# A decode kernel's last twenty microseconds: products ahead of sums, earlier output products, v-stationary tokens and unused matmuls

## The chip, the cores and the metric

The kernel runs on one core of a Trainium2 chip. The metric is the device time of one execution in microseconds (us), quoted as the median of several executions. The profile is of one execution, recorded by the hardware profiler; its "span" is 1.7 to 2.9 us shorter than the device time of the same execution. Points of time inside an execution are counted from the start of the span. The engines are called by their names in the profile: PE is TensorE's matmuls, PEld its weight loads, DVE VectorE, ACT ScalarE, SPq the queue of SyncE, which issues the DMA transfers. The "granted clock" (PEclk) is the share of TensorE's full clock that the throttle let through.

## The reference, cut to what matters

Two attention blocks, A and B, of the same shape, each with one query token, 32 heads, 8192 cached keys and values of 128 elements, all bf16. The outputs are concatenated.

```python
q = (x @ wq)                                     # [32 heads, 128]
scores = einsum("bhqd,bhkd->bhqk", q, k_cache) * 128 ** -0.5
p = softmax(scores)
o = einsum("bhqk,bhkd->bhqd", p, v_cache)
y = o.reshape(1, 1, 32 * 128) @ wo               # wo [4096, 512]
# ... once for A, once for B
out = concatenate([y_A, y_B], axis=-1)
```

The caches are 4 x 67 MB and everything is read once, so the data read decides the time: 285 MB.

## The kernel before: the parts that matter

Heads are taken two at a time: pair j, 0 to 31, of which 16 to 31 are B's. A pair's k (4 MB) and v (4 MB) go through a ring of five slots. For a pair j the kernel makes the elementwise products of k and q on DVE (`plan_M`, eight of 1.2 us), folds 128 elements to 8 on TensorE with an identity (`plan_fold`, two of 16 matmuls), sums the rest on DVE (`plan_R`), finds the maximum, takes the exponentials on ACT, and multiplies with v on TensorE (`plan_PV`). Work of neighbouring pairs is interleaved by hand. Every engine runs its own list in order. This is the order of one pair:

```python
for j in range(NPR):                  # NPR = 32
    plan_M(j, 0); plan_M(j, 1)
    plan_R(j - 1, 1); plan_m1(j - 1)  # second sum and maximum of the pair before
    plan_ri(j - 2)
    plan_M(j, 2); plan_M(j, 3)
    plan_tr(j - 1)
    plan_fold(j, 0)
    plan_ot(j - 2)                    # not for j = 31
    plan_M(j, 4); plan_M(j, 5)
    plan_m2(j - 1); plan_bc(j - 1); plan_exp(j - 1)
    plan_M(j, 6); plan_M(j, 7)
    plan_o(j - 2)                     # not for j = 31
    plan_R(j, 0)
    plan_fold(j, 1)
    plan_sum(j - 1)
    plan_PV(j - 1)                    # not for j = 30 and 31
    if j == LE:                       # LE = 28
        ... plan_w(0, ...)            # the weights of A's y, for each block of heads
        ... plan_y(0, ...)            # A's y: 32 matmuls of 512 columns
    if LE <= j < NPR - 1:
        plan_w_ready(j - 2)           # the weights of B's first 16 heads, for j = 28
```

`plan_PV` has p as the stationary operand and streams v, 4 tokens to a matmul of 512 columns. It needs a copy of its sum by ACT and then a turn on TensorE (`plan_ot`, 4 float32 matmuls that the profile counts as 8). `plan_PVturned` has v as the stationary operand, one token to a matmul of 2 columns, and adds to the turned sum directly. The end of the kernel before:

```python
LAST_PARTS = [(0, 64), (64, 96), (96, 128)]   # v of pair 31 comes in three transfers
NLW = 2                                       # the first two go through plan_PV
# ... behind the loop, j = 31:
plan_PV(j - 2); plan_tr(j); plan_ot(j - 2); plan_m2(j); plan_bc(j); plan_exp(j); plan_o(j - 2)
# ... then 96 matmuls of B's y (24 heads), the rest of the weights, the row sums, 16 more matmuls of y
plan_PV(j - 1)
plan_ot(j - 1)
plan_o(j - 1)
LW = LAST_PARTS[NLW - 1][1]
for i, (t0, t1) in enumerate(LAST_PARTS):
    W('PE', *part_of[i])                      # wait for this transfer
    if t1 <= LW:
        plan_PV(j, t0, t1, LW)
    else:
        if t0 == LW:
            plan_ot(j, False)
        plan_PVturned(j, t0, t1)
    if i == 0:
        plan_ysq(0)                           # y of pair 30's heads: 8 matmuls of 128 columns
plan_o(j)
plan_ysq(1)                                   # y of pair 31's heads, then the cast and the output
```

## Time and profile before

| what | before |
|---|---|
| median (lowest to highest) | 672.63 us (672.29 to 672.79, 3 runs) |
| read | 285.21 MB at 425 GB/s over the span |
| chain that ended last | DMA 62%, PE 24%, DVE 11% |
| last piece of v31 lands | 665.6 us |
| from there to the end of the cast | 3.8 us |

Below are three lines of the page: the span, and the clock and the DMA's busy share in 40 slices of the span, in tenths.

```profile
span 671.3 us, 6004 instructions
...
PEclk9998876779877767888876789877767888798787
DMA  9999999999999999999999999999999999999995
```

The DMA engines are busy throughout, so the stream sets when the last bytes land: in each of the seven profiles in which TensorE waited for the last landing (before, E2, E5 to E8 and E15 below) it came between 665.3 and 665.8 us. The clock row shows a TensorE that is cold (slowed by the throttle) for part of nearly every slice. The profile is of an execution of 673.07 us, 0.3 us above the three timed ones.

The end of the chain of waits of the kernel before, in order of time; the columns are start, length and what it was.

```profile
635.32 30.26 DMA ring<-in_B_v_cache_dram
...
665.62 1.26 PE stps L552 x8
666.89 0.87 PE stps L564 x32
...
667.85 0.19 DVE sq L585
...
668.08 1.03 PE qwps L689 x8
...
669.13 0.28 DVE y_sb L699
```

Here the chain runs back from the cast to a transfer: TensorE waited for the last third of v31. L552 is the turn, L564 the 32 v-stationary matmuls, L689 the output sum.

The windows view of the kernel before shows steps of 4 us; PEclk and the DMA share are the columns ahead of the last.

```profile
core 0: us, PE busy (x) PEld busy (x) DVE busy (x) ACT busy (x) POOL busy (x), PEclk, DMA share, GB/s
652.00:656.00 4.00, 3.70 (x113) 3.40 (x113) 0.52 (x3) 0.99 (x5) 0.00 (x0) 0.58 0.92 385
656.00:660.00 4.00, 3.79 (x33) 1.28 (x25) 0.00 (x0) 0.17 (x1) 0.00 (x0) 0.56 0.97 410
```

And this is the timeline of the kernel before, 65 us earlier, where A's y (L643) is made:

```profile
590.09 7.07 PE L643 MATMUL yps<-ring,w_bf 128*1 128x512 bf16 x32 [1.76 <-DVE w_bf L623]
...
597.68 0.42 DVE L614 TENSOR_TENSOR wt<-qwps,hmask 128x256 f32<-128x256 f32 x1 [7.74 <-PE qwps L607]
...
598.48 2.35 DVE L422 TENSOR_TENSOR ring<-ring,qbc 128x2048 bf16<-128x2048 bf16 x2
```

DVE is idle for 7.74 us. The product that it is waiting for (L607) makes the weights of B's first 16 heads, and it stands behind A's y on TensorE. Only then come the products of pair 29 (L422, 598.48 us), and they do not wait for k of pair 29 either.

### The profile page before, as it was taken

To read this page: it belongs to the slowest core of one execution; us is meant where nothing else is said; L and a number is where in the kernel's file an instruction comes from. 1 tells how busy PE (TensorE), PEld (TensorE's weight loads), DVE (VectorE), ACT (ScalarE), POOL (GpSimd) and SP (SyncE) were. 2 spreads that over 40 slices of the span, in tenths; PEclk is the share of its full clock that TensorE was granted. 3 is DMA by queue.
4 is the path that set the end of the run, shared out by engine and by line. 5 is a ranking of instruction groups with operands and counts; after the bars stand their busy time and mean duration, and the time that the engine had idled before them with its cause. 6 is when DMAs were issued, how large, how long until landed. Compare 5 with 4: busy or idle time off the path is not lost.

```text
span 671.3 us, 6004 instructions
## 1 busy us (share of the span) xinstructions
PE 439.0 (65%) x2782; PEld 102.8 (15%) x1822; DVE 387.5 (58%) x517; ACT 61.9 (9%) x203; POOL 2.4 (0%) x16
## 2 busy tenths in 40 slices
PE   2765775655677666567765655777566567757696
PEld 0200110101111010111111101111011111121134
DVE  5194566665555666555566665556666555555840
ACT  0101101001111001111100011110101111101010
POOL 1000000000000000000000000000000000000000
PEclk9998876779877767888876789877767888798787
DMA  9999999999999999999999999999999999999995
GB/s 375 437 437 433 430 421 431 437 436 432 421 428 437 437 433 430 420 435 437 433 435 428 424 435 437 433 433 422 430 437 435 433 428 424 433 436 429 426 422 240
DMA packets 10953, 285.38 MB, mean 425 GB/s; under 512 B 1211, under 2 KB 1726, under 8 KB 1854
## 3 DMA queue, kind: packets, MB, share of 16 engines
q1 hardware_dynamic: 10936, 285.22, 99.0%
q8 instruction: 8, 0.13, 0.1%
q14 instruction: 3, 0.02, 0.0%
q10 hardware_dynamic: 6, 0.00, 0.0%
HBM read 285.21 MB, written 0.00 MB: 425 GB/s over the span
## 4 chain that ended last, share of the span: by engine, by line
DMA 62%; PE 24%; DVE 11%; issue 2%; SPq 0%; DVEq 0%
DMA ring<-in_B_k_cache_dram 30%; DMA ring<-in_A_k_cache_dram 28%; PE fold L181 15%; DVE ring L422 8%; DMA ring<-in_B_v_cache_dram 5%; PE otps L526 3%; PE fold L177 2%; PE stps L552 1%; DVE s_sb L448 1%; PE yps L643 1%; DVE m L459 1%; PE stps L477 1%; DVE wt L614 0%; DVE w_bf L623 0%; DVE rinv L502 0%
## 5 line engine op out<-in xcount | busy, mean ns | idle before, releaser
L422 DVE TENSOR_TENSOR ring<-ring,qbc 128x2048 bf16<-128x2048 bf16 x256 | 298.4, 1216 | 166.5 <-DMA ring<-in_A_k_cache_dram 93.7
L181 PE MATMUL fold<-ring,ident 128*128 128x512 bf16 x960 | 276.3, 452 | 0.0
L467 PE MATMUL stps<-ident_f,m 128*2 128x128 f32 x32 | 11.1, 348 | 141.7 <-DVE rinv L502 140.2
L177 PE MATMUL fold<-ring,ident 128*128 128x512 bf16 x64 | 31.4, 491 | 64.6 <-DVE ring L422 64.6
L526 PE MATMUL otps<-ring,p 128*8 128x512 bf16 x1016 | 62.7, 387 | 0.2 <-DMA ring<-in_B_v_cache_dram 0.2
L552 PEld LDWEIGHTS stps<-sel,o 128*128 128x128 f32 x256 | 33.6, 192 | 157.3 <-issue 152.1
L448 DVE TENSOR_REDUCE s_sb<-fold 128x64 f32<-128x512 f32 x64 | 44.0, 688 | 3.2 <-PE fold L181 2.6
L483 ACT COPY nb<-stps 128x1 f32<-128x1 f32 x32 | 5.1, 159 | 419.2 <-PE stps L477 419.2
L585 DVE TENSOR_TENSOR ot<-stps,rinv 128x2 f32 (+1 forms) x30 | 4.8, 160 | 62.5 <-PE stps L552 62.5
L552 PE MATMUL stps<-sel,o 128*128 128x2 f32 x256 | 30.9, 243 | 3.1 <-DMA ring<-in_B_v_cache_dram 1.9
L541 ACT COPY o<-otps 128x512 f32<-128x512 f32 x32 | 18.7, 585 | 135.7 <-PE otps L526 135.7
L489 ACT ACTIVATE p<-s_sb,nb 64x128 bf16<-64x128 f32 x64 | 28.0, 437 | 3.8
L496 PEld LDWEIGHTS stps<-rowsum,ones_f 128*128 128x128 f32 x64 | 12.3, 194 | 98.7 <-issue 97.9
L467 PEld LDWEIGHTS stps<-ident_f,m 128*2 128x2 f32 x32 | 2.6, 81 | 158.8 <-DVE m L459 132.0
L526 PEld LDWEIGHTS otps<-ring,p 128*8 128x8 bf16 x1016 | 22.5, 87 | 24.3 <-issue 1.6
L387 PE MATMUL qwps<-ring,xsel 128*128 128x512 bf16 x64 | 18.6, 443 | 9.3 <-ACT qbc L394 4.8
L459 DVE TENSOR_REDUCE m<-s_sb 64x1 f32<-64x128 f32 x64 | 17.9, 280 | 2.1
L177 PEld LDWEIGHTS fold<-ring,ident 128*128 128x128 bf16 x64 | 6.4, 99 | 78.0 <-issue 59.6
L614 DVE TENSOR_TENSOR wt<-qwps,hmask 128x512 f32<-128x512 f32 (+3 forms) x5 | 2.2, 441 | 21.4 <-PE qwps L607 21.3
L477 PE MATMUL stps<-m,sel 2*128 2x1 f32 x64 | 12.1, 256 | 0.0
L489 ACT ACTIVATION_READ_ACCUMULATOR p<-s_sb,nb 64x1 f32 x64 | 11.6, 181 | 0.0
L477 PEld LDWEIGHTS stps<-m,sel 2*128 2x128 f32 x64 | 9.4, 182 | 10.5 <-issue 10.0
(49 smaller groups left out, 80.1 us busy)
## 6 DMA issues: line engine op xcount, KB each, us to landing
ring<-in_A_k_cache_dram SPq DMA_DIRECT2D x16, 4096.0 KB, 39.4
ring<-in_A_v_cache_dram SPq DMA_DIRECT2D x16, 4096.0 KB, 31.9
ring<-in_B_k_cache_dram SPq DMA_DIRECT2D x16, 4096.0 KB, 39.4
ring<-in_B_v_cache_dram SPq DMA_DIRECT2D x15, 4096.0 KB, 32.0
ring<-in_A_wq_dram SPq DMA_DIRECT2D x1, 4096.0 KB, 12.1
ring<-in_B_wq_dram SPq DMA_DIRECT2D x1, 4096.0 KB, 21.4
ring<-in_A_wo_dram SPq DMA_DIRECT2D x1, 4096.0 KB, 39.9
ring<-in_B_wo_dram SPq DMA_DIRECT2D x1, 2048.0 KB, 34.6
```

The lines of the kernel that those rows point to most:

```text
L177: return e.matmul(out, lhsT, rhs, start=start, stop=stop)
L181: return e.add_instruction(mybir.InstMatmult(name=nc.get_next_instruction_name(), engine=e.engine, ins=[e.lower_ap(rhs), e.lower_ap(lhsT)] ...
L387: m = e.matmul(qw_ps[:, :].rearrange("p (j d) -> p j d", d=Dh), xsel[:, a, c, par, :], wq[:, c, 4 * g:4 * g + 4, par, :], start=(i == 0), ...
L422: m_val[(j, i)] = INC('DVE', c_m, lambda e: e.tensor_tensor(t, t, qbc[:, at(j, 1), :].broadcast_to([P, CH, Dh]), ALU.mult))
L448: r_val[(j, h)] = INC('DVE', c_r, lambda e: e.tensor_reduce(s_sb[:, j % NS, h * HT:(h + 1) * HT], fold_ps[h][:, :].rearrange("p (t e) -> p ...
L459: m1_val[j] = INC('DVE', c_m1, lambda e, h=h, q0=q0, q1=q1: e.tensor_reduce(m1[q0:q1, j % NS, h:h + 1], s_sb[q0:q1, j % NS, :], AX.X, ALU. ...
L467: tr_val[j] = INC('PE', c_tr, lambda e: e.transpose(st_ps[0][0:2, 0:P], m1[:, j % NS, :], ident_f[:]))
L477: bc_val[j] = INC('PE', c_bc, lambda e: e.matmul(st_ps[0][:, P:P + 1], sel2[:], m2[0:2, j % NS:j % NS + 1], start=True, stop=True))
L489: e_val[j] = INC('ACT', c_e, lambda e, h=h, q0=q0, q1=q1: e.activation(p2[q0:q1, j % NS, :, h], s_sb[q0:q1, j % NS, :], AF.Exp, bias=nb[q0 ...
L526: m = e.matmul(ot_ps[j % NS % 2][32 * g:32 * g + 2 * TB, :], p2[:, j % NS, i:i + TB, :].rearrange("p t h -> p (t h)"), t[:, i:i + TB, :].r ...
L541: cp_val[j] = INC('ACT', c_cp, lambda e: e.copy(o8[:, j % NS % 2, :], ot_ps[j % NS % 2][:]))
L552: m = e.matmul(st_ps[1][:, 0:2], o8[:, j % NS % 2, i * Dh:(i + 1) * Dh], sel8[:, 2 * i:2 * i + 2], start=(i == 0), stop=(last and i == TB ...
```

## The change

It has four parts, all in the last two pairs. The products of pair 31 go on DVE ahead of the sums of pair 30, so that the last folds come earlier. The first 96 matmuls of B's y go between those folds. In pair 31 tokens 64 to 127 are v-stationary (before, 96 to 127) and come in pieces of 32, 16 and 16, so that the turn does not stand behind the last landing. And `plan_fill(n)` puts n unused matmuls of 512 columns at nine places in TensorE's list (29 in all: 15 ahead of PV of pair 30, 14 behind it), to keep its clock up.

```diff
-        LAST_PARTS = [(0, 64), (64, 96), (96, 128)]
-        NLW = 2
+        LAST_PARTS = {NPR - 1: [(0, 64), (64, 96), (96, 112), (112, 128)]}
+        NLW = 1
 ...
+        def plan_fill(n):
+            W('PE', c_r, r_val[(NPR - 1, 1)])
+            def op(e):
+                for i in range(n):
+                    (held_matmul if i else matmul)(
+                        e, fold_ps[0][:, :], ident[:],
+                        xsel[:, 0, 0:2].rearrange("p c k m -> p (c k m)"), start=True, stop=True)
+            OP('PE', op)
 ...
-        for j in range(NPR):
+        for j in range(NPR - 1):
 ...
+            if j == NPR - 2:
+                plan_M(j + 1, 0)
+                plan_M(j + 1, 1)
 ...
         j = NPR - 1
+        plan_M(j, 2)
+        plan_M(j, 3)
+        plan_R(j - 1, 1)
+        plan_m1(j - 1)
+        plan_ri(j - 2)
+        plan_fold(j, 0)
+        plan_tr(j - 1)
+        plan_M(j, 4)
+        plan_M(j, 5)
+        early = [b for b in perm_l if b[0] in w_done]
+        for b in early:
+            plan_y(LA, *b[:2])
+        plan_m2(j - 1)
+        plan_bc(j - 1)
+        plan_exp(j - 1)
+        plan_R(j, 0)
+        plan_M(j, 6)
+        plan_M(j, 7)
+        plan_fold(j, 1)
 ...
         plan_tr(j)
+        plan_fill(3)
         plan_ot(j - 2)
 ...
         plan_o(j - 2)
-        for b in early:
-            plan_y(LA, *b[:2])
+        plan_fill(5)
 ...
+        plan_fill(7)
         plan_PV(j - 1)
+        plan_fill(3)
         plan_ot(j - 1)
         plan_o(j - 1)
-        ... (the loop over the parts)
+        plan_fill(2)
+        plan_ysq(0)
+        plan_fill(2)
+        for t0, t1 in LAST_PARTS[j][:NLW]:
+            plan_PV(j, t0, t1, LAST_PARTS[j][NLW - 1][1])
+        plan_fill(3)
+        plan_ot(j, False)
+        for i, (t0, t1) in enumerate(LAST_PARTS[j][NLW:]):
+            plan_PVturned(j, t0, t1)
+            if i < 2:
+                plan_fill(2)
         plan_o(j)
         plan_ysq(1)
```

## The prediction

> **What bounds the kernel now.** The DMA stream. The page shows 285.2 MB read at a mean of 425 GB/s, with the DMA row at 9 tenths or more in all but the last of 40 slices; the chain that ended last is 62% DMA. The Trainium skill, "DMA: Bandwidth & Descriptors", section "Where 436 GB/s comes from", gives 435 GB/s as the ceiling of the fabric; the slices here reach 437, so there is little left to gain in the stream. The issue of v of pair 31 still waits for the second fold of pair 30 (634.45 us) and has some 30 us of transfers queued ahead, so even a microsecond there would not show.
>
> **The exposed part** follows the last landing. In the chain of waits the last third of v31 lands at 665.58 us. Then come: turning the bulk sum (L552, 8 matmuls) 1.26 us; 32 matmuls with v stationary 0.87 us; the scaling on DVE 0.19 us; 8 matmuls of the output sum 1.03 us; the cast, done at 669.41; the output transfer; end at 671.3. Cast end minus landing is 3.83 us.
>
> **What the change does there.**
> 1. Only tokens 0 to 63 go through the p-stationary path, so the turn can finish before the last landing: -1.26 us.
> 2. The last piece is 16 tokens, not 32: half of 0.87 us, about -0.4 us.
> 3. The unused matmuls (29 of 512 columns) should hold the clock up. In the windows view the granted clock fell from 1.00 to 0.50 within 652 to 653 us, returned after some 3.5 us of PV, and was 0.50 again from 667 on. The Trainium skill, "TensorE: Matmul & The Clock Gate", Part 1, says that an idle window of about 3.4 us halves the clock; the trace agrees, and the 1-column matmuls of y seem not to count as busy. The output sum took 0.61 us warm (662.31) against 1.01 us cold (668.08): up to -0.4 us.
> 4. The products of pair 31 moved ahead, and early y of B (2.65 us) between the folds, bring the last fold forward by an estimated 2 us (products 1.17 us each). Not on the path: v30 lands near 655.7 us, and PV of pair 30 waits for it either way.
> 5. Warm, PV of pair 30 should take 1.9 us instead of 3.8 us, so that TensorE has caught up before each v31 piece.
>
> Added: two smaller transfers for one larger, their landings near 664.35 and 665.6 us (estimate from 2.45 us per MB). Two fills ahead of the last piece cost 0.45 us warm, 0.85 us cold, and could delay it by 0.3 us.
>
> Sum: cast end minus landing from 3.83 to about 1.95 us; less some friction, -1.8 us: **670.8 us**, 8 in 10 between 670.0 and 671.9. Chance of faster by over 2%: 0.005; within 2%: 0.99; slower by over 2%: 0.005.
>
> **What would show it.** DMA rate and last landing of v31 unchanged (665.6 within 0.3). The last turn ends before the last landing; 16 stationary-v matmuls follow it; output sum near 0.6 us; clock near 1.0 from 655 to the end; second fold of pair 31 ends near 645.6 instead of 647.6.
>
> **What would make it wrong.** The fills are not paced: they run at once, and the gap until v30 lands may still cool the clock; then PV stays at 3.8 us, the turn of v31 slips towards 665 us and up to 1 us is lost. The last landing may shift by run noise (the three runs span 0.5 us), or the two small wo transfers issued last may land after the output sum could start.

## More of the kernel before

The timeline of the kernel before, where PV of pair 30 (L526) begins. In brackets stands the idle time ahead of it and what ended that.

```profile
655.40 0.16 ACT L670 COPY y_bulk<-yps 128x4 f32<-128x4 f32 x1 [2.54 <-PE yps L652]
...
655.75 0.60 PE L526 MATMUL otps<-ring,p 128*8 128x512 bf16 x3
...
655.99 3.80 PE L526 MATMUL otps<-ring,p 128*8 128x512 bf16 x29
```

PV of pair 30 has no bracket: TensorE came to it from its own work and did not wait for v of pair 30.

## The result, and the profile after

The changed kernel took 673.75 us (median of 4 runs, 672.29 to 675.05); the kernel before, in the same rounds, 672.59 us. The ratio is 1.0017, with a 95% interval of 0.9995 to 1.0039, so no change is shown, and the time lies outside the predicted 670.0 to 671.9. A ratio here is the mean time of one kernel's fast runs over that of the other's in the same rounds, so it is not quite the ratio of the medians. Besides the median, the spread changed: 2.8 us against 0.5 us. The profile that follows is of the slowest of the four, 675.05 us.

The span and the DMA row of the changed kernel's page:

```profile
span 673.2 us, 6087 instructions
...
DMA  9999999999999999999999999999999999999994
```

The end of its chain of waits (L531 is PV, L557 the turn, L570 the v-stationary matmuls, L695 the output sum, fold L177 and L181 the unused matmuls):

```profile
656.31 0.59 PE qwps L680 x2
656.90 0.54 PE fold L177
657.44 2.17 PE fold L181 x6
659.61 1.83 PE otps L531 x32
...
664.71 0.97 PE otps L531 x16
...
666.43 0.99 PE stps L557 x8
667.42 0.80 PE stps L570 x32
...
669.56 0.42 PE stps L570 x16
...
670.31 1.03 PE qwps L695 x8
```

There is no DMA line in this chain at all: in this execution TensorE waited for no landing from 656 us to the end. The seven unused matmuls at 656.90 took 2.7 us, because they ran cold, and held up PV of pair 30 until 659.6 us. The turn of pair 31 ended at 667.4 us. It was predicted to end before the last landing, but the four pieces of v31 were issued between 637.4 and 639.2 us and the last two took 26.4 us to land (the list of DMA issues of the same profile, median), so the last piece lay there from about 665.3 us on, waiting for TensorE. The data came on time and TensorE was late.

The windows of the changed kernel over the same stretch:

```profile
652.00:656.00 4.00, 3.91 (x39) 2.39 (x33) 0.88 (x5) 1.47 (x6) 0.00 (x0) 0.96 0.89 381
656.00:660.00 4.00, 3.75 (x24) 0.43 (x19) 0.00 (x0) 0.16 (x1) 0.00 (x0) 0.62 1.00 420
```

And A's y with what follows, in code that is the same in both kernels:

```profile
591.51 8.39 PE L649 MATMUL yps<-ring,w_bf 128*1 128x512 bf16 x32 [1.76 <-DVE w_bf L629]
...
600.43 0.42 DVE L620 TENSOR_TENSOR wt<-qwps,hmask 128x256 f32<-128x256 f32 x1 [9.07 <-PE qwps L613]
...
601.23 2.35 DVE L425 TENSOR_TENSOR ring<-ring,qbc 128x2048 bf16<-128x2048 bf16 x2
```

The products of pair 29 began 2.75 us later than in the profile of before (601.23 against 598.48 us). Of this, 1.3 us is A's y itself (8.39 against 7.07 us, in part at half clock). About 1.4 us more comes from the first fold of pair 28, whose last 15 matmuls took 6.08 us here, at a clock of 0.50 (window 576 to 580 us), and 4.54 us before, where the clock rose on the way (0.80 in the same window); k of pair 28 had landed at the same time in both (568.6 and 568.5 us). The Trainium skill, page "TensorE: Matmul & The Clock Gate", Part 1, says that the window over which the activity is judged runs freely and does not start anew with the kernel, so that the cold stretch varies from run to run. These traces are consistent with that (same code, same landing, 1.5 us difference in one fold), but no run shows the window itself; why one execution is colder than another is not shown here.

So two suspects stood against each other. Theory L: the chain of compute is late in some executions by clock luck far upstream, and the change needs a TensorE that is on time. Theory F: the unused matmuls lie on the path. There were two rivals: C, that the clock is what matters and the unused matmuls pay for themselves, and D, that the last landing or its split was harmed.

### The profile page after: what moved, and what is told of

Its sections match the earlier page's. It is cut to its first block, busy times and chain, and to the rows that moved or that the text cites. A ratio compares the mean times of both kernels' runs of the same rounds, so it can differ in the third digit from the quotient of the medians.

```text
span 673.2 us, 6087 instructions
## 1 busy us (share of the span) xinstructions
PE 446.8 (66%) x2832; PEld 103.2 (15%) x1855; DVE 387.5 (58%) x517; ACT 61.9 (9%) x203; POOL 2.4 (0%) x16
## 4 chain that ended last, share of the span: by engine, by line
DMA 58%; PE 28%; DVE 12%; issue 2%; SPq 0%; DVEq 0%; ACT 0%
DMA ring<-in_B_k_cache_dram 30%; DMA ring<-in_A_k_cache_dram 28%; PE fold L181 18%; DVE ring L425 8%; PE otps L531 4%; PE fold L177 2%; PE stps L557 2%; DVE s_sb L451 1%; PE yps L649 1%; DVE m L462 1%; PE stps L480 1%; DVE wt L620 0%; DVE w_bf L629 0%; DVE rinv L505 0%; PE stps L570 0%
## 5 line engine op out<-in xcount | busy, mean ns | idle before, releaser
L181 PE MATMUL fold<-ring,ident 128*128 128x512 bf16 x960 | 279.5, 456 | 0.0
L177 PE MATMUL fold<-ring,ident 128*128 128x512 bf16 x64 | 31.4, 490 | 64.1 <-DVE ring L425 64.1
L531 PE MATMUL otps<-ring,p 128*8 128x512 bf16 x1008 | 59.9, 379 | 0.0
L557 PEld LDWEIGHTS stps<-sel,o 128*128 128x128 f32 x256 | 33.4, 191 | 155.3 <-issue 152.6
L557 PE MATMUL stps<-sel,o 128*128 128x2 f32 x256 | 30.7, 242 | 0.0
L531 PEld LDWEIGHTS otps<-ring,p 128*8 128x8 bf16 x1008 | 21.6, 86 | 25.7 <-issue 3.0
L390 PE MATMUL qwps<-ring,xsel 128*128 128x512 bf16 x64 | 16.9, 411 | 9.4 <-ACT qbc L397 4.8
L177 PEld LDWEIGHTS fold<-ring,ident 128*128 128x128 bf16 x64 | 6.5, 101 | 78.6 <-issue 61.2
```

What stands on the lines that cost most here:

```text
L177: return e.matmul(out, lhsT, rhs, start=start, stop=stop)
L181: return e.add_instruction(mybir.InstMatmult(name=nc.get_next_instruction_name(), engine=e.engine, ins=[e.lower_ap(rhs), e.lower_ap(lhsT)] ...
L390: m = e.matmul(qw_ps[:, :].rearrange("p (j d) -> p j d", d=Dh), xsel[:, a, c, par, :], wq[:, c, 4 * g:4 * g + 4, par, :], start=(i == 0), ...
L531: m = e.matmul(ot_ps[j % NS % 2][32 * g:32 * g + 2 * TB, :], p2[:, j % NS, i:i + TB, :].rearrange("p t h -> p (t h)"), t[:, i:i + TB, :].r ...
L557: m = e.matmul(st_ps[1][:, 0:2], o8[:, j % NS % 2, i * Dh:(i + 1) * Dh], sel8[:, 2 * i:2 * i + 2], start=(i == 0), stop=(last and i == TB ...
```

## The experiments

Each ran five timed rounds beside the kernel before, plus the profiled execution, so 6 runs of each kernel, and 11 of the kernel before, which the runs of a call share. E1 to E8 ran on one chip in two calls, E9 to E12 on a second, E13 to E15 on a third. All outputs were correct.

| run | what | median us | lowest to highest | ratio to before, 95% interval |
|---|---|---|---|---|
| e1 | changed, no unused matmuls | 675.38 | 673.96 to 677.06 | 1.0035 [1.0010, 1.0060] |
| e2 | new order alone | 673.77 | 672.53 to 675.94 | 1.0015 [0.9990, 1.0040] |
| e3 | new parts of v31 alone | 676.35 | 673.10 to 676.73 | 1.0028 [1.0000, 1.0056] |
| e4 | changed, again | 673.54 | 671.77 to 674.77 | 1.0005 [0.9981, 1.0028] |
| e5 | before, B's weights ahead of A's y | 673.11 | 672.69 to 674.41 | 0.9996 [0.9976, 1.0016] |
| e6 | changed, B's weights ahead of A's y | 670.84 | 670.45 to 672.12 | 0.9961 [0.9941, 0.9981] |
| e7 | e6 less the 14 late unused matmuls | 671.67 | 671.08 to 672.12 | 0.9971 [0.9952, 0.9991] |
| e8 | e6 with v30 in parts, paced | 671.66 | 671.39 to 671.82 | 0.9971 [0.9952, 0.9990] |
| e9 | e6 without unused matmuls | 672.74 | 670.90 to 674.91 | 0.9993 [0.9970, 1.0016] |
| e10 | changed less the 14 late ones | 670.97 | 670.64 to 673.14 | 0.9973 [0.9953, 0.9993] |
| e11 | changed less the 7 ahead of PV of pair 30 | 671.99 | 671.59 to 673.56 | 0.9979 [0.9961, 0.9998] |
| e12 | e6, unused matmuls 4, 1, 2 at the end | 670.99 | 670.89 to 671.99 | 0.9967 [0.9950, 0.9984] |
| e13 | changed, same rounds as e14 and e15 | 673.06 | 671.05 to 674.09 | 0.9980 [0.9956, 1.0004] |
| e14 | as e10 | 671.84 | 671.45 to 672.93 | 0.9969 [0.9947, 0.9991] |
| e15 | as e6 | 671.12 | 670.66 to 672.37 | 0.9959 [0.9937, 0.9981] |

The kernel before, beside them: 672.70 us (672.15 to 676.15) and 672.80 (672.34 to 675.93) on the first chip, 673.93 (672.42 to 675.81) on the second, 674.37 (672.42 to 676.09) on the third. So the kernel before has late executions too, up to 676 us; the runs that came with it at first had happened to show none. All gains spoken of below are under 0.5%. Where an interval is given below for a difference of means, it is that of a t-test over the 6 and 6 runs.

### First call: the change taken apart

**E1: no unused matmuls.**

```diff
         def plan_fill(n):
+            return
```

> The changed kernel with every unused matmul taken out, all else kept. Theory F (the unused matmuls lie on the path, because TensorE, not the last landing, ends last: 2.7 us of 7 cold ones ahead of PV of pair 30, and about 1.5 us of later ones): 671.0 to 671.8 us, 1.5 to 2.5 us under the changed kernel, spread under 1 us. Rival C (the unused matmuls pay, and without them the clock is cold from 653 us): PV of pair 30 takes 3.8 us instead of 1.9, result equal to the changed kernel or slower, 673.5 us or more. Rival D (the last landing, or its split in four, is the cause): no change, 673.0 to 674.

Measured: 675.38 us, all six runs above 673.9. Theory F in its broad form fell: without the unused matmuls the kernel is slower than with them (673.54 us in the same rounds; by the means 2.2 us, 95% interval 0.6 to 3.8), not faster. Rival C had this right. The windows of E1's profile:

```profile
652.00:656.00 4.00, 1.48 (x24) 0.89 (x28) 0.35 (x3) 0.90 (x5) 0.00 (x0) 0.69 0.90 385
656.00:660.00 4.00, 3.48 (x32) 0.84 (x24) 0.00 (x0) 0.47 (x1) 0.00 (x0) 0.50 0.99 418
660.00:664.00 4.00, 3.50 (x27) 3.00 (x31) 0.18 (x1) 0.12 (x1) 0.00 (x0) 0.50 0.96 383
664.00:668.00 4.00, 3.30 (x36) 2.34 (x29) 0.00 (x0) 0.59 (x1) 0.00 (x0) 0.50 0.19 72
```

The clock stays at 0.50 from 655 us to the end. In this execution TensorE did wait for v of pair 30 (landed at 655.85 us), so it was on time, and still PV took 3.62 us and each turn 1.9 us instead of 1.0, and the cast ended at 671.03 us. Being cold alone costs the predicted gain.

**E2: the new order alone.** The order of products, folds and early y as in the changed kernel; the parts of v31 and the tail as before; `plan_fill` returns at once.

> Only the new order of the products, folds and early y; parts of v31 and the tail as before, no unused matmuls. Theory F: the order frees TensorE ahead of PV of pair 30, but the tail behind the last landing is the old one (3.8 us from landing to cast): 672.3 to 672.8 as before. If the order itself were the harm: above 673.2.

Measured: 673.77 us, 672.53 to 675.94, against 672.70 us; the ratio's interval holds 1, so neither side of the expectation is decided. In its profile the chain was as late as in the first profile of the changed kernel (products of pair 29 at 601.4 us), and TensorE nevertheless waited for the last landing, at 665.62 us. From the end of the second fold of pair 30 to the end of the second fold of pair 31 was 12.4 us here and in the changed kernel, 13.2 before: the new order won 0.8 us. The prediction had said 2 us. The missing part is clock again: the last 15 matmuls of that fold took 5.09 us after a gap, before 3.40.

E2's profile also separates lateness from unused matmuls, as it is as late as the first profile of the changed kernel but has none of them. This is its timeline where PV of pair 30 begins:

```profile
656.21 0.59 PE L531 MATMUL otps<-ring,p 128*8 128x512 bf16 x3
...
656.59 3.19 PE L531 MATMUL otps<-ring,p 128*8 128x512 bf16 x29
```

PV began at 656.2 us here, at 659.5 us in the changed kernel (same view) and at 655.75 us before. So of the 3.8 us by which the changed kernel came later, the 15 unused matmuls ahead of PV make 3.3; the lateness from upstream, less what the new order won, makes 0.5. In return PV was warm (1.90 us instead of 3.6 here), so that it ended 1.7 us later and not 3.3.

**E3: the new parts of v31 alone.** The old loop over all 32 pairs put back; four parts of v31 with 64 tokens v-stationary; `plan_fill` returns at once.

> Only the new parts of v31 (64 tokens with p stationary, then 32, 16 and 16 with v stationary); the order as before, no unused matmuls. Theory F: about 1.3 us shorter behind the landing as far as TensorE has caught up by then; PV of pair 30 cold (3.8 us) eats some of it: 671.2 to 672.3. Rival D: 673.0 to 674 as in the changed kernel, as it has the same four transfers.

Measured: 676.35 us, with two runs at 673.1 and four near 676.5. Missed: the shorter tail brought nothing. In the profile, one of the late runs, A's y took 10.0 us, PV of pair 30 began at about 659.7 us, and TensorE waited for no landing after it. A late TensorE cannot use a shorter tail, and a cold one is slow in it: each turn of 8 matmuls takes 1.05 us warm, and the last one here took 1.87 us.

**E4: the changed kernel again.**

> The changed kernel unaltered, for its spread on this chip and a second profile. All theories: 672.3 to 675.1 us. If the path runs through TensorE from the landing of k of pair 28 on, as the first profile has it, the time follows the start of PV of pair 30 (659.5 us in the first profile), while the last landing stays at 665.3 to 665.7 us.

Measured: 673.54 us, 671.77 to 674.77. Its profile is of an early execution: A's y took 7.07 us, the products of pair 29 began at 598.6 us. The chain is then 2.6 us ahead of the first profile, and so is the end, span 670.6 against 673.2 us. That is Theory L's mark. But it still ends without waiting for the last landing (chain of waits):

```profile
654.26 0.54 PE fold L177
654.80 2.18 PE fold L181 x6
656.98 1.83 PE otps L531 x32
...
667.67 1.03 PE qwps L695 x8
```

### Second call: the chain brought back on time

If lateness comes from A's y standing in front of B's weights, the cure is one line moved.

```diff
             if j == LE:
                 for h0, n, pm in wo_plan[0]:
                     plan_w(0, h0, n)
+            if LE <= j:
+                plan_w_ready(j - 2)
             if j == LE:
                 for h0, n, pm in wo_plan[0]:
                     plan_y(0, h0, n)
-            if LE <= j:
-                plan_w_ready(j - 2)
```

**E5: this in the kernel before.**

> The kernel before, with one thing moved: the weights of B's first 16 heads (4 instructions on DVE) are made ahead of the 32 matmuls of A's y, so that DVE no longer waits 7.1 to 10 us for those. Theory L (the late runs come from the serial chain of compute that begins with k of pair 28 and grows by what a cold clock adds; here it falls back on the landing of k of pair 29, by an estimate near 597.7 us): the late runs of 675.8 and 676.2 us vanish, 672.1 to 672.9 us in every run, spread under 0.8. Rival (the late runs come from elsewhere, or from the stream): late runs above 675 stay as frequent.

Measured: 673.11 us, 672.69 to 674.41; no run above 675, against two of eleven of the kernel before. Most of the expectation is missed: three of the six runs (673.42, 673.50 and 674.41 us) and the median lie above the 672.9 us that it allowed, and the spread is 1.7 us. Only the runs above 675 us are absent, and with six runs this is not shown to be more than luck: at the rate of the kernel before, two of eleven, six runs without one have a chance of about 0.3. (The profile shows two instructions on DVE moved, of 0.42 us each, not four.) The median did not fall, as expected, since this tail follows the last landing.

**E6: this in the changed kernel.**

> The changed kernel with the same move. Theory L plus F (TensorE ends last; the chain late by clock luck is most of the spread, the unused matmuls the rest): every run like the early profile of the changed kernel (670.6 us span), 671.4 to 672.4 us, spread under 1 us, and in the trace TensorE still waits for no landing after PV of pair 30. If only the lateness mattered (L without F): 670.5 to 671.2, with the last landing waited for. If neither: 673 to 675.

Measured: 670.84 us, ratio 0.9961 with the interval clear of 1. This is the predicted time. The timeline of E6 where the products of pair 29 begin, while A's y is still running beside them (9.84 us in this execution):

```profile
597.55 2.36 DVE L425 TENSOR_TENSOR ring<-ring,qbc 128x2048 bf16<-128x2048 bf16 x2 [5.71 <-DMA ring<-in_B_k_cache_dram]
```

Now DVE waits for k of pair 29 itself, so the lateness from before 597.5 us is gone, although A's y took longer than in any of the profiles above except E3's. The end of the chain of waits:

```profile
615.57 39.95 DMA ring<-in_B_v_cache_dram
...
655.57 1.90 PE otps L531 x32
...
662.46 0.99 PE stps L557 x8
...
665.09 0.45 PE fold L177
665.54 0.43 PE fold L181
665.97 0.42 PE stps L570 x16
...
666.71 1.02 PE qwps L695 x8
...
667.76 0.28 DVE y_sb L705
```

PV of pair 30 waits for its landing and runs warm, in 1.90 us. The turn of pair 31 ends at 663.5 us, before the last landing. The first weight load of the last 16 matmuls waits for their transfer, which is there by 665.47 us, but the two unused matmuls ahead of them run cold and end only at 665.97 us, so these two cost about 0.5 us in this execution (the prediction had allowed 0.3). The expectation had L with F end at 671.4 to 672.4 and L alone at 670.5 to 671.2: the median fits L alone, though two of the six runs lie above it and the spread is 1.7 us.

E5 and E6 ran in the same rounds and differ in the change alone, both with the move: 672.69 to 674.41 us against 670.45 to 672.12, by the means 2.2 us (95% interval 1.4 to 3.1). Without the move the same change brings nothing (E4 against the kernel before). So the change is worth what was predicted, if TensorE is on time.

**E7: E6 less the 14 unused matmuls behind PV of pair 30.**

```diff
-        plan_fill(3)                  # behind PV of pair 30
-        plan_fill(2)                  # on either side of plan_ysq(0)
-        plan_fill(2)
-        plan_fill(3)                  # ahead of the last turn
-            if i < 2:
-                plan_fill(2)          # between the last pieces
```

> As the one before, with the 14 unused matmuls behind PV of pair 30 taken out and the 15 ahead of it kept. Theory F: what they cost on the path (about 1.5 us by the early profile: 666.93 back to the last landing near 665.6) is won, as long as the clock stays up: 670.3 to 671.2 us. Rival C (they hold the clock up and so pay for themselves): the clock falls before 665 us, the turn takes 1.9 us instead of 1.0, 672 us or more.

Measured: 671.67 us against 670.84, between the two expectations; the intervals of the two ratios overlap for the most part. In its profile the clock stayed at 1.00 from 656 to 666 us and the last turn took 1.05 us, against rival C, and the last 16 matmuls began on their landing. With TensorE on time taking these 14 out wins nothing that shows.

**E8: an attempt at a better version.** v of pair 30 in four transfers, the first half of v31 in two, unused matmuls only where TensorE waits.

```diff
-        LAST_PARTS = {NPR - 1: [(0, 64), (64, 96), (96, 112), (112, 128)]}
+        LAST_PARTS = {NPR - 2: [(0, 32), (32, 64), (64, 96), (96, 128)],
+                      NPR - 1: [(0, 32), (32, 64), (64, 96), (96, 112), (112, 128)]}
 ...
+        for t0, t1 in LAST_PARTS[j - 1]:
+            plan_PV(j - 1, t0, t1)
+            if t0 >= 64:
+                plan_fill(2)
 ...
```

> An attempt at a version that beats both: the same move, v of pair 30 in four parts and the first half of v31 in two, each multiplied as it lands, and unused matmuls only where TensorE waits for a landing or a copy. Theory F: TensorE ends within 0.5 us of the last landing (665.6 us), 670.5 to 671.3 us in every run. If the stream suffers from the smaller transfers: the last landing after 666 us and no gain over the kernel before.

Measured: 671.66 us, with the smallest spread of all, 0.43 us. It is steady, but 0.4 us above its expected range. Its last 16 matmuls begin at 665.79 us, on the landing, and the clock is at 0.50 from 666 us on.

### Third call: what the unused matmuls are worth

**E9: E6 without any unused matmuls** (`plan_fill` returns at once).

> The changed kernel with B's first weights ahead of A's y (the version that gave 670.84 us) and with all 29 unused matmuls out. If the move alone made the gain (lateness was the whole cause): 670.3 to 671.2 us, as with them. If the unused matmuls are needed as well (theory C): clock 0.50 from 655 us to the end, PV of pair 30 about 3.6 us, TensorE behind the last landing, 673 to 675 us, as in the run without them before the move.

Measured: 672.74 us, 670.90 to 674.91. The median falls between the two expectations. Some executions are as quick as with them (the profiled one, 671.11 us, was warm from 660 us on), others are not. Against E12 of the same rounds, which has them, the mean is 1.5 us higher (672.76 and 671.25 us; 95% interval of the difference -0.3 to 3.3). So it is likely, and not shown beyond doubt, that the move alone is not the whole gain.

**E10: the changed kernel less the 14 late ones, without the move** (diff as in E7).

> The changed kernel, without the move, less the 14 unused matmuls behind PV of pair 30. Theory F in its narrow form (they cost only where the chain is late, as TensorE then waits for no landing): 672.0 to 673.0 us, 0.5 to 1.5 us under the changed kernel, although they cost nothing measurable with the move. If they hold the clock up: 673.5 us or more.

Measured: 670.97 us, four runs near 670.8 and two near 673.1; the median is below the expected range, on a chip on which the changed kernel was not run. Its profile is of an execution in which TensorE came to PV of pair 30 almost when it did in E4 (657.18 against 656.98 us), so the two show what the 14 cost on a late TensorE (chain of waits of E10):

```profile
654.99 2.19 PE fold L181 x6
657.18 1.86 PE otps L531 x32
...
664.32 1.74 PE stps L570 x64
...
666.39 0.62 PE qwps L695 x8
```

The output sum begins 1.28 us earlier than in E4 (666.39 against 667.67 us), and runs warm, in 0.62 instead of 1.03 us.

**E11: the changed kernel less the 7 ahead of PV of pair 30.**

```diff
-        plan_fill(7)
         plan_PV(j - 1)
```

> The changed kernel, without the move, less the 7 unused matmuls right ahead of PV of pair 30. They took 2.7 us there, cold, and PV of pair 30 then 1.9 us. Without them PV should start 1 to 2.7 us earlier but take 3.0 to 3.8 us: 672.8 to 674.0, no clear difference from the changed kernel. If they are a pure cost: under 672.

Measured: 671.99 us, 0.8 us under the expected range and at the edge of what was named for a pure cost, on a chip on which the changed kernel was not run. In its profile, of one of its two slow runs (673.42 us; the other four are at 671.6 to 672.1), PV of pair 30 began on its landing, 655.66 us, ran cold (3.58 us), and the clock was 1.00 only from 661 us. So without the 7 PV is cold; whether they cost more than they bring isn't decided.

**E12: E6 with more unused matmuls at the end.**

```diff
-            if i < 2:
-                plan_fill(2)
+            plan_fill((4, 1, 2)[i])
```

> The version that gave 670.84 us, with the unused matmuls between the last pieces set 4, 1 and 2 (behind the last piece, under the scaling on DVE) instead of 2, 2 and 0. If that keeps the clock up through the output sum (0.61 instead of 1.01 us): 670.3 to 670.7 us. If the clock falls anyway: 670.8 to 671.3.

Measured: 670.99 us on another chip, ratio 0.9967 against E6's 0.9961, above the 670.7 us that it allowed for a clock kept up, so no gain is shown. In its profile the clock did stay at 1.00 through the output sum, which took 0.55 us, but the sum began at 666.70 us, where E6's began at 666.71.

### Fourth call: on one chip, in the same rounds

E4 and E10 had run on different chips. Three runs settle these.

> The changed kernel unaltered, in the same rounds as the two that follow. All theories: 672.3 to 675 us with a spread of 2 us or more, ratio to the kernel before 0.999 to 1.002.

> The changed kernel less the 14 unused matmuls behind PV of pair 30, without the move. If those cost on the path whenever the chain is late (narrow form of F): 1.5 to 2.5 us under the changed kernel of the same rounds, with two groups of times, near 670.7 and near 673. If the difference between the earlier runs came from the chips: within 0.7 us of the changed kernel.

> The changed kernel with B's first weights ahead of A's y, all unused matmuls kept. Theory L: 670.4 to 672.1 us again, 2 us or more under the changed kernel of the same rounds, spread under 2 us. If the gain came from the chip or the rounds: within 0.7 us of the changed kernel.

Measured: 673.06, 671.84 and 671.12 us. The move (E15) takes 1.9 us off the changed kernel by the medians, just short of the 2 expected, and 1.6 by the means (95% interval 0.5 to 2.8), and its spread falls from 3.0 to 1.7 us: Theory L holds, and the chip is not the cause. Taking out the 14 late unused matmuls (E14) takes off 1.2 us by the medians and 0.9 by the means (95% interval -0.2 to 2.0), less than expected, so this part is likely and not shown beyond doubt. E14's profile suggests why it is not more: from 660 us to the end its clock was 0.50, so what it saved in matmuls it lost in part to the clock.

The version that beats both kernels is E6 and E15, the changed kernel with B's first weights ahead of A's y: ratios to the kernel before of 0.9961 and 0.9959, intervals clear of 1.

## Why the prediction was wrong, point by point

- **The stream bounds the kernel, and the change leaves it alone: right.** The DMA row is as full after as before, and wherever TensorE waited for the last landing it came at the same time: E2 at 665.62 us with three parts, E6 about 665.5 us with four. Rival D is out.
- **The step that failed is number 5 with the end of number 4.** It said of the last folds "Not on the path: v30 lands near 655.7 us, and PV of pair 30 waits for it either way", and "so that TensorE has caught up before each v31 piece". In the profile of before PV of pair 30 began at 655.75 us with no wait for a landing. That v30 landed at about the same time (655.85 us in E1) was a coincidence of one execution, and TensorE had no slack at all. In the changed kernel's first profile TensorE got there 0.7 us later, spent 2.7 us on unused matmuls, began PV 3.9 us later than before, and never caught up. The prediction took the 15 unused matmuls ahead of PV to fall into a wait for v30; there was none, and they made 3.3 of the 3.8 us (E2's profile). That they warmed PV to 1.90 us was right and did not make this good. E6 and E15, which put the chain back on a landing, gave 670.84 and 671.12 us against 670.8 predicted: the shortening of the tail was real, and the assumption that TensorE would be there to use it was wrong. From the last landing to the end of the cast, for which 1.95 us was predicted, E15's profile has about 1.9 us, and E6's, whose clock fell at 665 us, about 2.6.
- **Where the lateness comes from was not in the prediction.** It read the tail from one profile and took its upstream times as fixed. They are not: A's y took 7.07 to 10.0 us in different executions, the first fold of pair 28 4.5 to 6.1 us, and from the landing of k of pair 28 on, in the kernel before, nothing waits for a landing until 663 us. The kernel before is less exposed, because with its turn behind the last landing and no unused matmuls it has less to do between PV of pair 30 and that landing; still it has late runs of up to 676 us.
- **"The fills are not paced; the gap may still cool the clock": half right.** That was named among what could go wrong, and sized at up to 1 us. What was missed is that unused matmuls that run when TensorE is late are themselves on the path. The 14 late ones likely cost about 1 us that way (E13 against E14; 1.28 us up to the output sum in the profiles of E4 and E10). As a whole they still pay: without them 1.8 us more by the medians (E1 against E4).
- **Turn off the path, -1.26 us: right where TensorE is on time.** In E6 it ends at 663.5 us, 2 us before the last landing.
- **16 instead of 32 matmuls at the end, -0.4 us: right.** 0.87 us before, 0.42 us in E6 and after.
- **Output sum warm, -0.4 us: not reliable.** It took 1.0 us in the changed kernel's first profile, in E4 and in E6, 0.62 us in E10 and E15. The clock fell at 665 us in E6.
- **The new order brings the last fold forward by 2 us: mis-sized.** It measured 0.8 us, because the fold then runs cold (5.09 instead of 3.40 us).
- **The small transfers of wo landing too late: not seen.** No profile has a wait for them.

What stays open: no profile was taken of the slowest executions of the kernel before (above 674 us), so that they are late in the same way is argued and not shown. What points to it: all eight of its 44 runs above 675 us have a mean granted clock of 0.803 to 0.806, the other 36 of 0.807 to 0.818, and E3, which keeps the old order, was profiled in such a run (clock 0.806) with A's y at 10.0 us. Why the clock is lower in one execution than in another is open. What E5's one run of 674.41 us waited for is also not known.

## What to carry to other kernels

Before a tail behind the last landing is shortened, look at whether the engine that does it waits for that landing in the profile; an engine that starts its work "at the same time" as a landing but without a wait has no slack, and another execution may be late. Look far upstream for a place where an engine idles behind an instruction that it does not need, and move that first: here one move of that kind, 70 us before the end, let the change bring what it was made for. Unused matmuls that keep the clock up belong where TensorE waits; where it is late they are part of the path.

## What the Trainium skill lacked or had wrong

- "TensorE: Matmul & The Clock Gate", Part 1, says that the clock follows how busy the PE has been, but not which matmuls count; only transposes are named as not counting, in Part 4. In the kernel before, PE was busy for 3.70 of the 4 us from 652 to 656 us with matmuls of 1 column for the most part, and the granted clock was 0.58 there, having fallen to 0.50 at about 652.7 us, 3.1 us after the last matmul of 512 columns and with no idle stretch of such length. So the prediction's "the trace agrees" holds only if these small matmuls count as idle, which the page does not say. Busy time in the profile does not tell that the clock will hold.
- The same page, Part 1, puts the penalty of the ramp at under 1% of a typical span. Here the eight executions of the kernel before above 675 us, up to 4 us (0.6%) above the fastest, had a mean granted clock of 0.803 to 0.806, the others 0.807 to 0.818. That is within the page's figure, but twice the gain that was at stake.
- The same page's table of goals says to keep TensorE busy and to leave no gaps over about 3 us. It does not say that unused matmuls put in for that cost time when the engine is late: likely about 1 us for 14 of them here (E13 against E14), against 1.8 us that all 29 bring (E1 against E4).
- "DMA: Bandwidth & Descriptors", section "Where 436 GB/s comes from", gives a ceiling of 435.2 GB/s for the fabric. Slices of the kernel before show 437 GB/s, but the same profile books 524 GB/s for the single microsecond from 649 to 650, at a DMA share of 1.22, so a slice is no exact measure; the mean over the span is 425, and the page is not shown to be wrong.
